# A fused attention and SoLU feed-forward kernel: one load of k moved ahead of two loads of v and a store, one transposing transfer moved ahead of a store

## The chip, the cores and the metric

The kernel runs on one core of a Trainium2 chip. A core has a matrix engine (TensorE; PE in the profile, PEld for its weight loads), VectorE (DVE), ScalarE (ACT), GpSimd (POOL), and SyncE (SP), which in this kernel issues every DMA transfer, in one queue and in program order. The metric is the device time of one launch in microseconds (us), lower is better.

## The reference

For 8 batches of 8 heads (576 rows, head size 64) the reference computes a linear attention, and on its output a feed-forward layer with the SoLU activation and a layer norm:

```
q_s = softmax of q over the head dimension; k_s = softmax of k over the rows
kv  = einsum('bhsd,bhse->bhde', k_s, v)
x   = einsum('bhsd,bhde->bhse', q_s, kv), as 4608 x 512
h   = x @ w_in                       (512 -> 1024)
s   = h * softmax(h)
ln  = (s - mean) / sqrt(var + 1e-6) * g_ln
out = ln @ w_out                     (1024 -> 512)
```

All inputs and the output are float32.

## The kernel before

Work is cut into pieces, and each piece is a Python generator: at each `yield` it stops, and the next call emits its next few instructions. The string `ORDER` names the generators one after another; `K4*3` means three steps of K4, and a suffix such as `.v` puts a step's movable instruction on VectorE. Since scheduling is manual, ORDER is the program order, so each engine's instructions run in the order in which the steps name them, and SP's transfers too. An instruction whose input isn't ready holds up all that stand behind it on its engine. Where instructions on different engines depend on each other, semaphores are put in automatically.

A number in a name below is a batch (0 to 7) for the first five kinds, and a row tile of 128 output rows for the others (36 tiles; four or five per batch).

- `LKb` (`load_keys`, L248): one transfer of 1152 KB that brings the batch's k into the tile `km`. There is one such tile, so the transfer waits until the kv products of batch b-1 have read the old one.
- `Vbi` (`load_v`, L228): a transfer of 288 KB for one of four parts of v into `vm`. There is one `vm` too, so each waits for the kv products of the batch before.
- `Kb` (`keys`): the softmax of k and the kv product, 26 steps. Steps 1 to 3 take the maximum over the rows on VectorE (`khalf`, L445 and L447, one step each; then `ktop`, L449 and L450); then come the transposes of the maximum, the subtraction (L456), the exponential (L458), the products into `kv` (L470), the normalization and a power of two as scale. The last six steps split the result into two float16 halves in `bd`: for each half of the partitions a scaled copy on ScalarE (L499), a copy on ScalarE (L501) and the remainder on VectorE (L503).
- `Qba`, `Qbc` (`queries`): the softmax of q for two row tiles, split into float16 halves in `qhl` (L547 computes the low half on GpSimd). The last step is only a transposing transfer, `qT<-qhl` (L574, on SP).
- `LQb` (`load_queries`): loads of q.
- `xt` (`attend`, L665): the attention product of two row tiles from `qT` and `bd`; then ScalarE and VectorE bring it out of PSUM.
- `Ht` (`hidden_twin`, L733): h = x @ w_in for two row tiles by seven block products. Its sums pass through the tile `vw`: ScalarE or VectorE copies a block out of PSUM into one half of `vw` (L171 or L173), VectorE adds it to another block and takes the maximum (L759, L769, L771), and a later copy overwrites the half. A product that adds onto a PSUM block can start only when the block has been copied.
- `ht` (`hidden`): softmax, product, mean and variance of a tile, ending in the transposing transfer `uT<-u` (L858).
- `ot` (`project`): 7 steps: a scale; four steps of products with w_out (L1117); the scaling out of PSUM into `os` (L1130 on ScalarE); the store to the output (L1133, on SP). Two `os` buffers are used in turn.

Around the first place of the change ORDER has, in order, V52, the last kv products of K4, V53, V50, the store of o7, LK5, the first two steps of K5, the last three steps of K4, the transposing transfer of Q4a and then a step of H15 whose first instruction is L759. Around the second place it has the store of o14 (the last of `o14*2`) and, eight steps on, the last step of Q5c.

Of the kernel before, what the change touches and what calls it, by code (L numbers as in the profile page):

```python
# [17 lines left out]
P = 128  # L18
# [27 lines left out]
}  # L46
ORDER = (
# [51 lines left out]
)  # L99


# [1153 lines left out]
```

## Time and profile before

| | us |
|---|---|
| median of 3 runs | 436.26 (436.16 to 440.52) |
| the profiled execution, device time | 436.4 |
| its span, first to last instruction | 434.6 |
| TensorE busy | 414.3 (95%) |
| VectorE busy | 379.2 (87%) |
| ScalarE busy | 333.5 (77%) |
| GpSimd busy | 315.1 (72%) |

The granted clock of TensorE is 1.0 of full speed in every slice of the span. The rows come from one profiled execution; start times are counted from the start of its span, which is 1.8 us shorter than its device time.

### The profile page before, as it was taken

The numbers are of one execution on the slowest core, as the hardware profiler recorded it, in microseconds if no ns is written. First come the engines' busy times: TensorE is split into PE (matmuls) and PEld (weight loads), VectorE is DVE, ScalarE is ACT, GpSimd is POOL, SyncE is SP. The second block draws the span as 40 slices with busy tenths as digits, with TensorE's granted clock in tenths as the row PEclk, the third lists the DMA queues.
The fourth block names the chain that finished last, engine by engine and source line by source line (L and its number), as shares of the span: only waits on it lengthen the run. The fifth ranks groups of instructions, "written<-read, shape, count | busy, mean of one in ns | idle before, by whom it ended". The sixth has DMA issues, their size and how long they took to land.

```text
span 434.6 us, 9274 instructions
## 1 busy us (share of the span) xinstructions
PE 414.3 (95%) x3473; PEld 221.0 (51%) x3473; DVE 379.2 (87%) x765; ACT 333.5 (77%) x566; POOL 315.1 (72%) x329
## 2 busy tenths in 40 slices
PE   2699999999999999989999999999999999999996
PEld 1444534454445444534544445445444558676885
DVE  5999999999889999976979968999999999896862
ACT  2789998786877889748865767898889878965830
POOL 4208765899899769848888799789998875687520
PEclk9999999999999999999999999999999999999999
DMA  8989895699897996687899686999424957769993
GB/s 275 409 308 330 180 200 137 123 220 226 180 203 146 238 206 136 157 159 160 184 201 205 92 205 117 278 228 120 110 50 97 142 104 137 151 136 183 167 229 113
DMA packets 185900, 78.72 MB, mean 181 GB/s; under 512 B 165240, under 2 KB 174720, under 8 KB 185856
## 3 DMA queue, kind: packets, MB, share of 16 engines
q1 hardware_dynamic: 185856, 78.14, 80.5%
q8 instruction: 27, 0.44, 0.4%
q14 instruction: 17, 0.14, 0.1%
HBM read 36.70 MB, written 9.44 MB: 106 GB/s over the span
## 4 chain that ended last, share of the span: by engine, by line
PE 73%; DVE 9%; DMA 8%; ACT 5%; issue 2%; SPq 2%; POOL 1%; DVEq 0%; ACTq 0%
PE o L1117 23%; PE h L733 19%; PE h L810 12%; PE kv L470 3%; DMA qm<-in_q_dram 3%; PE o_2y L1048 3%; PE x L665 2%; DMA km<-in_k_dram 2%; PE o_0y L1048 2%; PE o_2z L1048 2%; PE o_2x L1048 2%; DMA qT<-qhl 1%; PE o_0z L1048 1%; PE o_0x L1048 1%; DMA uT_2c<-u_2c 1%
## 5 line engine op out<-in xcount | busy, mean ns | idle before, releaser
L1117 PE MATMUL o<-wo,uT 128*128 128x512 f16 x576 | 130.8, 379 | 0.2 <-ACT os L1130 0.2
L1117 PEld LDWEIGHTS <-uT 128*128 128x128 f16 x576 | 55.1, 98 | 67.3 <-issue 2.9
L810 PE MATMUL h<-wi,xT 128*128 128x512 f16 x240 | 53.6, 379 | 0.0
L733 PE MATMUL h<-wt,split 128*128 128x512 f16 x198 | 46.1, 379 | 0.4 <-ACT vw L171 0.3
L547 POOL TENSOR_TENSOR qhl<-qm,qhl 128x512 f16<-128x512 f32 x28 | 34.5, 1250 | 15.5 <-ACT qhl L171 15.4
L733 PEld LDWEIGHTS <-split 128*128 128x128 f16 x264 | 25.5, 98 | 32.1 <-issue 2.8
L810 PEld LDWEIGHTS <-xT 128*128 128x128 f16 x240 | 23.3, 98 | 28.1 <-issue 0.7
L522 POOL TENSOR_TENSOR qm<-qm,qnmx 128x1024 f32<-128x1024 f32 (+1 forms) x15 | 28.6, 1915 | 6.2 <-DVE qnmx L520 5.9
L456 POOL TENSOR_TENSOR km<-km,kb 128x1152 f32<-128x1152 f32 x12 | 31.5, 2628 | 0.9 <-issue 0.6
L733 PE MATMUL h<-wi,xT 128*128 128x512 f16 x132 | 30.6, 379 | 0.0
L733 PEld LDWEIGHTS <-xT 128*128 128x128 f16 x198 | 19.2, 98 | 21.7 <-issue 0.4
L802 PE MATMUL h<-iw,xT 128*128 128x512 f32 x64 | 29.3, 599 | 0.9 <-ACT e L865 0.9
L540 POOL TENSOR_TENSOR qm<-qm,qrec 128x1024 f32<-128x1024 f32 x13 | 25.0, 1921 | 2.9 <-DVE den L477 1.0
L520 DVE TENSOR_REDUCE qnmx<-qm 128x16 f32<-128x1024 f32 (+1 forms) x17 | 19.2, 1144 | 3.9 <-DMA qm<-in_q_dram 3.9
L171 ACT COPY vw<-h 128x512 f32<-128x512 f32 x25 | 14.6, 584 | 9.9 <-DVE top L759 6.7
L824 ACT ACTIVATE e<-h,nm,hs 128x1024 f32<-128x1024 f32 x18 | 21.6, 1201 | 0.4
L524 ACT ACTIVATE qm<-qm 128x1024 f32<-128x1024 f32 (+1 forms) x17 | 17.0, 999 | 6.1 <-POOL qm L522 6.1
L470 PEld LDWEIGHTS kv<-vm,km 64*64 64x64 f32 x1152 | 18.0, 134 | 6.3 <-ACT km L458 3.1
L470 PE MATMUL kv<-vm,km 64*64 64x65 f32 x1152 | 19.5, 219 | 1.7 <-ACT km L458 1.6
L1130 ACT ACTIVATE os<-o,rr 128x512 f32<-128x512 f32 x22 | 15.1, 686 | 7.7 <-PE o L1117 7.2
L458 ACT ACTIVATE km<-km 128x1152 f32<-128x1152 f32 x16 | 18.2, 1161 | 2.9 <-POOL km L456 2.7
L865 ACT ACTIVATE e<-h,nmu 128x1024 f32<-128x1024 f32 x14 | 15.6, 1114 | 5.9 <-DVE u L855 5.7
(330 smaller groups left out, 1072.7 us busy)
## 6 DMA issues: line engine op xcount, KB each, us to landing
km<-in_k_dram SPq DMA_DIRECT2D x7, 1152.0 KB, 7.8
vm<-in_v_dram SPq DMA_DIRECT2D x28, 288.0 KB, 4.0
out_dram<-os SPq DMA_DIRECT2D x31, 256.0 KB, 3.0
qm<-in_q_dram SPq DMA_DIRECT2D x7, 1024.0 KB, 6.7
wo<-in_moe_w_in_dram SPq DMA_DIRECT2D x4, 512.0 KB, 8.5
w_in<-in_moe_w_in_dram SPq DMA_DIRECT2D x4, 512.0 KB, 9.2
wo<-in_moe_w_out_dram SPq DMA_DIRECT2D x4, 512.0 KB, 5.7
w_out<-in_moe_w_out_dram SPq DMA_DIRECT2D x4, 512.0 KB, 8.9
```

Source lines behind the costliest of these rows:

```text
L456: on(nc.gpsimd).tensor_tensor(km[:, ns], km[:, ns], wide, op=ALU.subtract)
L470: nc.tensor.matmul(o, km[half, n, c], vm[half, n, c], start=(m == 0 and c == 0), stop=(m == 1 and c == KC - 1))
L520: nc.vector.tensor_reduce(shaped(nmx), x, axis=AX.X, op=ALU.max, negate=True)
L522: on(nc.gpsimd).tensor_tensor(x, x, wide(nmx), op=ALU.add)
L540: on(nc.gpsimd).tensor_tensor(x, x, wide(rec), op=ALU.mult)
L547: on(nc.gpsimd).tensor_tensor(lo, y, hi, op=ALU.subtract)
L733: nc.tensor.matmul(out, lefts[left](s, i), right_block(right, r, i), start=(n == 0 and not onto), stop=(n + 1 == len(terms)), skip_group_c ...
L802: nc.tensor.matmul(h[:, ns], xT[:, kc], iw[kc][:, ns], start=(i == 0), stop=(i == NP - 1))
L810: nc.tensor.matmul(h[:, ns], xT[:, t, kc], wi[:, s, kc, ns], start=(i == 0), stop=(i == len(terms) - 1))
L824: nc.scalar.activation(e, h, AF.Exp, bias=nm, scale=hs, accum_out=z)
L1048: nc.tensor.matmul(accs[acc], t[:, j, first + f], out_block(right, s, f), start=(f == n == 0 and not onto), stop=(f + 1 == NF // 2 and n = ...
L1117: nc.tensor.matmul(o, uT[:, j, f], wo[:, s, f, cols], start=(f == 0 and j == 0 and s == 0), stop=(f == NF - 1 and j == 1))
```

## The change

Only the string ORDER is changed. LK5 moves from behind o7's store and K4's next-to-last group of steps to a place right behind the last kv products of K4, that is, in front of V53, V50 and the store of o7. The last three steps of K4, which stood behind the first two steps of K5, now stand in front of them. The store of o14 moves from in front of `h18.v` to behind the last step of Q5c, which is that batch's second transposing transfer of q. All other steps keep their order. Line breaks apart, the diff is:

```
-  x15 K4 V53 Q4c*2 x15 V50 Q4a*2 H13*3 Q4a K4*2 o11.v
+  x15 K4 LK5 V53 Q4c*2 x15 V50 Q4a*2 H13*3 Q4a K4*2 o11.v
...
-  x15 K4*5 H15*2 H15.v H15*2 K4 LK5 K5*2 K4*3 Q4c Q4a H15*3 K5
+  x15 K4*5 H15*2 H15.v H15*2 K4*4 K5*2 Q4c Q4a H15*3 K5
...
-  x22 o14*2 h18.v h18 K6.v H20 h19 o15 h18 x22 Q5c h19
+  x22 o14 h18.v h18 K6.v H20 h19 o15 h18 x22 Q5c o14 h19
```

## Rows read from the trace of the kernel before

**Rows 1.** The page, part 1: busy us, share of the span, instructions.
```profile
PE 414.3 (95%) x3473; PEld 221.0 (51%) x3473; DVE 379.2 (87%) x765; ACT 333.5 (77%) x566; POOL 315.1 (72%) x329
```
**Rows 2.** Waits of TensorE: waiting line, releaser, us in total, times, longest.
```profile
PE h L733 <- ACT vw L171: 2.1, 2, 1.8
...
PE x L665 <- DMA qT<-qhl: 0.5, 1, 0.5
```
**Rows 3.** Window: length, busy us PE, PEld, DVE, ACT, POOL, clock, DMA share, GB/s.
```profile
195.40:250.20 54.80, 54.80 (x421) 25.74 (x420) 47.32 (x109) 41.48 (x77) 45.25 (x50) 1.00 0.80 168
```
**Rows 4.** Chain that ended last, 172 to 206 us: start, us, what.
```profile
182.89 8.51 DMA km<-in_k_dram
...
194.76 0.59 ACT vw L171
```
**Rows 5.** Timeline of SP, 179 to 192 us: start, us, line, operation.
```profile
179.56 0.59 SPq L228 DMA_DIRECT2D vm<-in_v_dram  x1
...
180.20 1.71 SPq L228 DMA_DIRECT2D vm<-in_v_dram  x1
181.97 0.81 SPq L1133 DMA_DIRECT2D out_dram<-os  x1
...
183.39 7.90 SPq L574 DMA_TRANSPOSE qT<-qhl  x1
```
**Rows 6.** Timeline of VectorE, 188 to 195 us; in brackets idle before, and releaser.
```profile
188.53 1.00 DVE L503 SCALAR_TENSOR_TENSOR bd<-kvn,s_kv,bd 64x256 f16<-64x256 f32 x1 [0.30 <-ACT bd L499]
191.42 1.23 DVE L445 TENSOR_TENSOR khalf<-km 128x1024 f32<-128x1024 f32 x1 [1.90 <-DMA km<-in_k_dram]
192.68 0.69 DVE L447 TENSOR_TENSOR khalf<-khalf 128x512 f32<-128x512 f32 x1
193.41 0.48 DVE L503 SCALAR_TENSOR_TENSOR bd<-kvn,s_kv,bd 64x256 f16<-64x256 f32 x1
193.92 0.70 DVE L759 CUSTOM_DVE_ANT_0 h<-h,vw 128x512 f32<-128x512 f32 x1
```
**Rows 7.** Timeline of ScalarE near 189 us.
```profile
188.94 0.50 ACT L499 ACTIVATE bd<-kvn,s_kv 64x256 f16<-64x256 f32 x1
```
**Rows 8.** Timeline of TensorE, 192 to 198 us.
```profile
192.18 1.47 PE L733 MATMUL h<-wt,split 128*128 128x512 f16 x6
195.40 1.46 PE L733 MATMUL h<-wi,split 128*128 128x512 f16 x6 [1.75 <-ACT vw L171]
196.78 0.97 PE L665 MATMUL x<-qT,bd 128*64 128x256 f16 x16
```
**Rows 9.** Time to landing in three source views: L248 (k), L228 (v), L574 (qT).
```profile
DMA to landing us min/median/max: 5.3/7.4/8.5
...
DMA to landing us min/median/max: 3.2/4.0/9.4
...
DMA to landing us min/median/max: 4.3/4.7/9.9
```
**Rows 10.** Chain that ended last, 236 to 256 us.
```profile
243.83 0.69 ACT os L1130
...
245.01 5.73 DMA qT<-qhl
```
**Rows 11.** Timeline of GpSimd near 242 us.
```profile
241.71 2.28 POOL L547 TENSOR_TENSOR qhl<-qm,qhl 128x512 f16<-128x512 f32 x2
```
**Rows 12.** Timeline of TensorE, 248 to 252 us.
```profile
248.81 1.46 PE L733 MATMUL h<-wi,xT 128*128 128x512 f16 x6
250.78 0.97 PE L665 MATMUL x<-qT,bd 128*64 128x256 f16 x16 [0.51 <-DMA qT<-qhl]
```
**Rows 13.** Timeline of VectorE, 227 to 240 us.
```profile
227.28 1.48 DVE L445 TENSOR_TENSOR khalf<-km 128x1024 f32<-128x1024 f32 x1 [1.58 <-DMA km<-in_k_dram]
...
239.64 0.48 DVE L503 SCALAR_TENSOR_TENSOR bd<-kvn,s_kv,bd 64x256 f16<-64x256 f32 x1
```
**Rows 14.** Timeline of TensorE near 241 us.
```profile
241.42 0.97 PE L665 MATMUL x<-qT,bd 128*64 128x256 f16 x16
```

102 rows, old and new, of the table ORDER are left out of this document.

## The prediction

> **What bounds the kernel now.** I read the page first. TensorE is busy 414.3 of 434.6 us [rows 1], and the chain that ended last is TensorE's for most of its length: time can be won only where TensorE stands idle. So the next view is the list of what TensorE waited for. The longest are at the kernel's start, which the change doesn't touch; in its middle two waits are left [rows 2]: the product of `hidden_twin` (L733) for a ScalarE copy into `vw`, longest 1.8 us, and the attention product (L665) for the transfer of a `qT`, 0.5 us. A window from the end of the first to the start of the second says that nothing else is open between them: TensorE is busy for the whole 54.80 us [rows 3].
>
> The next views are the chain of waits at each place, and the engines' timelines around it. The first wait starts with the load of the sixth batch's k (`km`): it is issued at 182.89 and lands 8.51 us later, at 191.40 [rows 4]. SP could have issued it sooner. Its condition, the last kv product of batch 4, is met when V53 goes out at 179.56; then V50 (1.71 us) and a store (0.81) stand in front [rows 5]. On VectorE `khalf` (L445) sits idle 1.90 us for `km`, and behind it in program order come L447, a `bd` split (L503) and at 193.92 the maximum L759 [rows 6]. ScalarE may overwrite `vw` only then (194.76 [rows 4]), and TensorE, idle 1.75 us, goes on at 195.40 [rows 8].
>
> The second wait is SP's alone. The store of o14 waits for `os`, which ScalarE starts at 243.83, and only behind it Q5c's transposing transfer goes out at 245.01, to land 5.73 us later [rows 10]. GpSimd had its source `qhl` ready at 241.71 + 2.28 = 243.99 [rows 11]. TensorE idles 0.51 us [rows 12].
>
> **Part 1: LK5 in front of V53, V50 and o7's store; the last three steps of K4 in front of the first two of K5.** Nothing is added or removed; two queues see another order, SP's and VectorE's (ScalarE's share of K4 keeps its place among ScalarE's work).
>
> SP: `km` goes out at about 179.6 instead of 182.9. The nine loads of k take 5.3 to 8.5 us to land (median 7.4) [rows 9]; so this one lands between 184.9 and 188.1. V53, V50 and the store go out behind it, each later by its issue of about half a microsecond or by as long as the queue holds them back. V53 and V50 are read by the kv products of batch 5, which need that batch's whole chain of key steps first, and that chain begins with the very `khalf` of [rows 6]; this hides the delay.
>
> VectorE: the second L503 moves ahead of `khalf`. The first one ends at 188.53 + 1.00 = 189.53 [rows 6]; the second needs the L499 that ran on ScalarE from 188.94 for 0.50 [rows 7], so it can run at about 189.56, and with 0.48 it ends at 190.04. The new order is then 190.07 `khalf` (1.23), 191.33 L447 (0.69), 192.05 L759. That is 1.87 earlier than 193.92. Even the latest landing, 188.1, is 1.9 us ahead of `khalf`: k is off the path, and VectorE's own queue is what remains.
>
> ScalarE copies `vw` 0.84 us behind the start of L759 (193.92 to 194.76), TensorE follows 0.64 us later: 192.05 + 1.48 = 193.53. Without any wait TensorE would be there at 192.18 + 1.38 = 193.56, where 1.38 is the step from one group of six products to the next work, 195.40 to 196.78 [rows 8]. So the wait ends at the same time as the work before it: the gain is 195.40 - 193.56 = 1.84 us. It is a near tie, so bounds: one VectorE operation may take half a microsecond more, as the first L503 did beside the second (1.00 against 0.48 [rows 6]), which leaves 1.3; the plain durations of these very instructions are the nearest rows, so I take 1.84. At worst the load still lands at 191.4 and only L503 is out of the way (0.5), or another transfer pays for it (below zero; rival D).
>
> Later work must come forward with it. ScalarE, GpSimd and VectorE near 195 to 200 all stand behind this copy or behind TensorE's product, so they move too.
>
> The one transfer that a quicker TensorE may overtake is Q4a's: issued at 183.39, its issue lasting 7.90 us [rows 5], and landed 9.9 us after (the maximum of its kind [rows 9]), at 193.3. Its reader, the L665 group now at 196.78, would start at 194.9. That is 1.6 us of cover. The trace shows that this transfer, put behind k, was held until k was nearly in. The Trainium skill ("DMA: Bandwidth & Descriptors", section "Queues, rings and completion order") says that each DMA engine takes its descriptors in ring order; by that rule two pieces of v and a store now stand between k and this transfer, which is where rival D has its place. The row agrees with the rule as far as k is concerned. Against it counts that the same bytes stand ahead of the transfer before and after; only their order changes.
>
> **Part 2: Q5c's transfer in front of o14's store.** The transfer goes out at 244.0, when `qhl` is ready, not at 245.01. With its own 5.73 us it lands at 249.7, with the median of 4.7 [rows 9] at 248.7. TensorE without a wait would want it at 248.81 + 1.38 = 250.19 instead of 250.78 [rows 12]: gain 0.59 us, bounds 0.51 (the idle time as the row counts it) and 0. The store goes out some microseconds later; its `os` buffer is one of two, and the next output tile to be scaled (o15) writes the other, so a whole tile's projection hides the delay and I cost it at nothing; without that cover it would be the delay itself, up to the 5.73 us that the transfer takes. Since both sides of this race come forward by the same 1.84 us, the gains add.
>
> **Sum.** 1.84 + 0.59 = 2.43 us off the profiled execution's 436.4 (span 434.6, 1.8 around it): 434.0. The median of the runs shown, 436.26, is 0.14 lower; I leave that inside the range. This is 0.5%, below the 1% that a measurement of this kernel can tell from no change.
>
> **The rivals.**
> A. The forecast: both waits go and all later work moves, 433.4 to 434.6.
> B. Part of the first gain is taken back later. The next place where VectorE, not TensorE, sets the pace begins with LK6: `khalf` at 227.28 had waited 1.58 us for it, and VectorE is full from there on [rows 13]. If that load doesn't come forward, the `bd` split of batch 5 still ends at 239.64 + 0.48 = 240.12 [rows 13], while its reader, the L665 at 241.42 [rows 14], wants to start at 239.58: 0.54 us lost. With the tie of part 1 lost as well (0.54) the time is 436.4 - 2.43 + 1.1 = 435.1. For it: the transfer engines are 80% busy in this stretch [rows 3]. Against it: it is issued behind work of GpSimd that itself moves forward.
> C. The change doesn't do what it says: k, put ahead, shares its way with the pieces of v and still lands at about 191.4. Then L759 gains only the 0.5 of the L503 that no longer stands between, and part 2 remains: 436.4 - 0.5 - 0.59 = 435.3. Against it: that would be 11.8 us, 3.3 over the longest of nine.
> D. Slower. Place: the L665 group at 194.9, which waits for Q4a's transfer. V50, now behind k and V53, is held back on SP for as long as that transfer was (7.90 us [rows 5]): it goes out at about 180.8 and frees SP at 188.7, the store takes 0.8, and Q4a's transfer starts only at 189.5 instead of 183.39. With the median landing (4.7) it is there at 194.2 and costs nothing; with the 9.9 that it needed before, at 199.4, and TensorE stands 4.5 us: 436.4 - 2.43 + 4.5 = 438.5. It costs from a landing at 194.9 on and ends on the slower side from 197.3. For it: V50 was already held for 1.71 us with only V53 ahead, which itself took 0.59 [rows 5]. Against it: those 9.9 us were spent behind k, and k would be in by then.
> E. More than forecast: a small idle time further on goes too, 433.0.
>
> **How the numbers follow.** A 0.64, B 0.18, C 0.06, D 0.07, E 0.05. The predicted time is A's, 434.0. The range runs from E's edge, 432.9, to 436.6, which takes in B and C and leaves the larger part of D and surprises out. Faster by over 1% would be below 431.9, which no case gives: 0.02. Slower by over 1% would be above 440.6; D would need another 2.1 us: 0.03. Within 1%: 0.95.
>
> **What would show it.** Right: `km` of batch 5 issued near 179.6 and landed before 189; no idle time for DMA ahead of that `khalf`; the two rows of TensorE's waits [rows 2] gone or below 0.2 us; the transfer of Q5c issued within 0.1 us of `qhl`'s end; the end of the span 2.2 to 2.6 us earlier. Wrong: a wait of L665 for `qT` near 195 (D), a `khalf` that still waits for k (C), or TensorE idle between 230 and 290 (B).

## The result and the profile after

The changed kernel takes 433.86 us (median of 11 runs, 433.66 to 434.79); the kernel before, measured beside it, 437.89 (11 runs, 435.66 to 440.52). The ratio is 0.991, 95% interval 0.989 to 0.994. The profiled execution takes 433.8 us against 436.4, its span 432.0 against 434.6. The forecast was 434.0, that is a ratio of 0.994 to the profiled 436.4, just outside this interval: the measured gain is the larger one.

So the two profiled executions differ by 2.6 us, as forecast (2.43), but the two medians by 4.0. In 19 of 86 runs of the kernel before, taken over the three later measurements, the mean granted clock of TensorE was 0.996 or lower, and these are 19 of its 25 times above 437.3; for the 11 runs here, six of them above 437.3, the clock isn't on record.

In the changed kernel's own lines, numbers are two higher (L733 is L735, and so on). The waits of TensorE from 70 us to the end, which answer to [rows 2] (waiting line, releaser, us in total, times, longest):

```profile
PE h L735 <- ACT vw L173: 0.3, 1, 0.3
```

Both waits that the forecast was about are gone; the 0.3 us that is left lies near 349 us and was there before, as the shorter of the two waits in the first row of [rows 2]. The timeline of SP, which answers to [rows 5], and in the second fence k's landing from the DMA view (KB each, us from issue to landing):

```profile
175.67 0.60 SPq L230 DMA_DIRECT2D vm<-in_v_dram  x1
179.63 0.40 SPq L250 DMA_DIRECT2D km<-in_k_dram  x1
180.08 2.97 SPq L230 DMA_DIRECT2D vm<-in_v_dram  x2
183.09 3.57 SPq L1135 DMA_DIRECT2D out_dram<-os  x1
186.76 2.64 SPq L576 DMA_TRANSPOSE qT<-qhl  x1
```

```profile
km<-in_k_dram SPq DMA_DIRECT2D x1, 1152.0 KB, 7.0
```

k goes out at 179.63 and lands at 186.6. Behind it SP is held up: the two pieces of v take 2.97 us to issue, the store 3.57. VectorE's timeline (against [rows 6]) and, in the second fence, TensorE's (against [rows 8]):

```profile
188.54 1.53 DVE L505 SCALAR_TENSOR_TENSOR bd<-kvn,s_kv,bd 64x256 f16<-64x256 f32 x2 [0.29 <-ACT bd L501]
190.10 1.23 DVE L447 TENSOR_TENSOR khalf<-km 128x1024 f32<-128x1024 f32 x1
191.36 0.69 DVE L449 TENSOR_TENSOR khalf<-khalf 128x512 f32<-128x512 f32 x1
191.97 0.69 DVE L761 CUSTOM_DVE_ANT_0 h<-h,vw 128x512 f32<-128x512 f32 x1
```

```profile
192.19 1.47 PE L735 MATMUL h<-wt,split 128*128 128x512 f16 x6
193.50 1.46 PE L735 MATMUL h<-wi,split 128*128 128x512 f16 x6
194.89 0.97 PE L667 MATMUL x<-qT,bd 128*64 128x256 f16 x16
```

No bracket stands behind `khalf` any more: VectorE finds k there, 3.5 us after it landed, and what it waits for is its own queue. TensorE's group that started at 195.40 starts at 193.50, with its predecessor at the same time as before (192.18, now 192.19): 1.90 us gained.

The second place: the timelines of SP, of GpSimd (the low half of `qhl`) and of TensorE, a fence each, against [rows 10], [rows 11] and [rows 12]:

```profile
242.01 1.66 SPq L576 DMA_TRANSPOSE qT<-qhl  x1
243.76 1.20 SPq L1135 DMA_DIRECT2D out_dram<-os  x1
```

```profile
239.71 2.28 POOL L549 TENSOR_TENSOR qhl<-qm,qhl 128x512 f16<-128x512 f32 x2
```

```profile
246.91 1.46 PE L735 MATMUL h<-wi,xT 128*128 128x512 f16 x6
248.30 0.97 PE L667 MATMUL x<-qT,bd 128*64 128x256 f16 x16
```

The transfer goes out 0.02 us after its source is ready (239.71 + 2.28 = 241.99). The attention product starts at 248.30 instead of 250.78: 2.48 us, of which 1.90 came from the first place and 0.58 are new. That carries to the end, where the span is 2.6 us shorter.

### The profile page after: what moved, and what is told of

Same layout as the page of the kernel before. It is cut to its first block, busy times and chain, and to the rows that moved or that the text cites. A ratio compares the mean times of both kernels' runs of the same rounds, so it can differ in the third digit from the quotient of the medians.

```text
span 432.0 us, 9275 instructions
## 1 busy us (share of the span) xinstructions
PE 414.5 (96%) x3473; PEld 221.6 (51%) x3473; DVE 378.8 (88%) x765; ACT 333.6 (77%) x566; POOL 316.1 (73%) x329
## 4 chain that ended last, share of the span: by engine, by line
PE 82%; DVE 8%; DMA 3%; ACT 2%; issue 2%; POOL 1%; SPq 0%; DVEq 0%; ACTq 0%; POOLq 0%
PE o L1119 26%; PE h L735 21%; PE h L812 12%; PE kv L472 4%; PE x L667 3%; PE o_2y L1050 3%; PE o_2z L1050 2%; PE o_0y L1050 2%; PE o_2x L1050 2%; PE h L804 2%; PE o_0z L1050 1%; PE o_0x L1050 1%; DMA uT_2c<-u_2c 1%; DVE qnmx L522 1%; DMA qm<-in_q_dram 1%
## 5 line engine op out<-in xcount | busy, mean ns | idle before, releaser
L735 PE MATMUL h<-wt,split 128*128 128x512 f16 x198 | 46.1, 379 | 0.5 <-ACT vw L173 0.3
L735 PEld LDWEIGHTS <-split 128*128 128x128 f16 x264 | 25.5, 98 | 30.2 <-issue 0.8
L735 PE MATMUL h<-wi,xT 128*128 128x512 f16 x132 | 30.6, 379 | 0.0
L735 PEld LDWEIGHTS <-xT 128*128 128x128 f16 x198 | 19.2, 98 | 21.7 <-issue 0.4
```

What stands on the lines that cost most here:

```text
L735: nc.tensor.matmul(out, lefts[left](s, i), right_block(right, r, i), start=(n == 0 and not onto), stop=(n + 1 == len(terms)), skip_group_c ...
```

## The experiments

All kernels but the last group are the kernel before with another ORDER. "At full clock" are the runs with a mean granted clock of 0.998 or more.

| kernel | median (range), us | ratio to before [95%] | runs, of these below full clock | median at full clock |
|---|---|---|---|---|
| before, three measurements together | | | 86, 19 | 436.34 |
| both parts | 434.18 (433.73 to 435.02) | 0.994 [0.992, 0.996] | 9, 1 | 434.03 |
| part 1 | 434.58 (433.90 to 435.75) | 0.995 [0.993, 0.997] | 12, 0 | 434.58 |
| part 2 | 436.68 (435.06 to 439.30) | 1.001 [0.998, 1.003] | 12, 5 | 436.01 |
| load moved, no swap | 434.19 (433.63 to 434.29) | 0.993 [0.991, 0.996] | 7, 0 | 434.19 |
| swap, load not moved | 436.07 (435.06 to 438.53) | 0.997 [0.995, 0.999] | 12, 2 | 435.70 |
| V51 too in front of k | 438.63 (436.44 to 441.66) | 1.004 [1.001, 1.006] | 12, 8 | 436.80 |
| the same again | 436.70 (435.46 to 440.85) | 1.002 [0.999, 1.005] | 12, 4 | 436.26 |
| k behind V53 and V50 | 434.49 (433.90 to 437.44) | 0.995 [0.992, 0.997] | 12, 1 | 434.38 |
| V51 in front of Q4a's transfer | 434.11 (433.59 to 435.01) | 0.993 [0.991, 0.996] | 7, 1 | 434.07 |
| before, wait filled | 436.43 (435.84 to 437.85) | 1.000 [0.998, 1.002] | 12, 1 | 436.32 |
| V51 in front of k, wait filled | 436.77 (436.26 to 438.81) | 1.001 [0.999, 1.003] | 12, 0 | 436.77 |

**Both parts together**, measured beside the parts.

> Both parts of the change. Theory (two exposed waits removed): 433.9 us, profile as the changed kernel's: k of batch 5 lands near 186.6, no wait of TensorE between 70 and 290 us. Theory on spread: runs of the kernel before scatter over 435.7 to 440.5 because TensorE waits there for transfers whose landing varies; with both waits gone all runs lie within 1.2 us. Rival on spread: the scatter has another source, so it shows here too.

434.18 us with a scatter of 1.3 us (1.2 expected), beside a kernel before at 435.33 to 439.66. The difference of the full-clock medians is 436.34 - 434.03 = 2.31 us; that of all runs of this measurement is 436.42 - 434.18 = 2.24, so the 4.0 us of the first measurement did not come again. k landed at 180.80 + 5.7 = 186.5, the expected number, but that is a coincidence: in this trace all of this stretch runs 1.2 us later than in the changed kernel's, and the load took 5.7 us instead of 7.0. TensorE has no wait of more than 0.3 us between 70 and 433 us in it.

**Part 1 alone.**

```diff
-  x15 K4 V53 Q4c*2
+  x15 K4 LK5 V53 Q4c*2
...
-  K4 LK5 K5*2 K4*3 Q4c
+  K4*4 K5*2 Q4c
```

> Part 1 alone (k in front of V53, V50 and o7's store, the last steps of K4 in front of K5's first). Theory: 1.84 to 1.9 us below the kernel before's profiled 436.4, so 434.5; the wait of L665 for qT near 249 stays at 0.5 us. Rival (the store's place is what counts): 435.8 or more. Spread: small if k's landing is its source, as wide as before if the second wait is.

434.58. TensorE, timeline at the second place:

```profile
248.87 0.97 PE L665 MATMUL x<-qT,bd 128*64 128x256 f16 x16 [0.46 <-DMA qT<-qhl]
```

The wait for `qT` is still there, as expected (0.46 against 0.51 [rows 12]). The rival is out, since all 12 runs lie below its 435.8.

**Part 2 alone.**

```diff
-  x22 o14*2 h18.v h18
+  x22 o14 h18.v h18
...
-  x22 Q5c h19
+  x22 Q5c o14 h19
```

> Part 2 alone (Q5c's transfer in front of o14's store). Theory: 0.6 us below 436.4, so 435.8; k of batch 5 still lands near 191.4 and TensorE still waits 1.75 us near 195. Rival (the transfer would have been hidden once anything moves): no gain, 436.4. Spread: as wide as before if k's landing is its source.

In the trace it does what it should; TensorE's waits from 70 us on are one row:

```profile
PE h L733 <- ACT vw L171: 2.2, 2, 1.9
```

The wait for `qT` has gone, the one for `vw` stays. But the time, 436.68, can't be told from before (ratio 0.998 to 1.003): 0.6 us is lost in the scatter, and 5 of these 12 runs were below full clock. At full clock it is 436.01, 0.3 below the kernel before. The part's worth is read from the traces, 0.5 to 0.6 us (the wait that is gone, and the product that starts at 248.87 with part 1 alone and at 248.30 with both), not from these times. The five runs can't be the edit's doing if the clock falls near 197 us, as in the traces below, since the edit takes effect near 244; the kernel before beside it has 1 such run in 27. So the share of such runs seems to vary by itself.

**The load without the swap.**

```diff
-  x15 K4 V53 Q4c*2
+  x15 K4 LK5 V53 Q4c*2
...
-  K4 LK5 K5*2 K4*3 Q4c
+  K4 K5*2 K4*3 Q4c
```

> Only LK5 moved; K5's first two steps stay in front of K4's last three. Theory (the load is what was late, and VectorE's work ahead of L759 is the same in either order): khalf starts at 189.6, L759 near 192.0, the same 1.84 us as part 1 alone: 434.5. Rival (the swap of the steps carries the gain): L759 stays near 193.9, 436.4.

434.19, the whole gain. VectorE's timeline:

```profile
188.65 1.01 DVE L503 SCALAR_TENSOR_TENSOR bd<-kvn,s_kv,bd 64x256 f16<-64x256 f32 x1 [0.30 <-ACT bd L499]
189.59 1.21 DVE L445 TENSOR_TENSOR khalf<-km 128x1024 f32<-128x1024 f32 x1
190.83 0.69 DVE L447 TENSOR_TENSOR khalf<-khalf 128x512 f32<-128x512 f32 x1
191.55 0.48 DVE L503 SCALAR_TENSOR_TENSOR bd<-kvn,s_kv,bd 64x256 f16<-64x256 f32 x1
192.07 0.70 DVE L759 CUSTOM_DVE_ANT_0 h<-h,vw 128x512 f32<-128x512 f32 x1
```

With k there in time the order of the four operations hardly matters: L759 starts at 192.07 here and at 191.97 with the swap. The swap rival is out.

**The swap without the load.**

```diff
-  K4 LK5 K5*2 K4*3 Q4c
+  K4 LK5 K4*3 K5*2 Q4c
```

> Only the swap: the last three steps of K4 in front of K5's first two, LK5 where it was (behind o7's store). Theory: k still lands near 191.4 and khalf starts then, but the L503 of 0.48 us no longer stands between khalf and L759, so L759 starts at 193.4, TensorE waits 1.25 instead of 1.75 us: 435.9. Rival (the swap carries the gain): 434.5. Rival (nothing without the load): 436.4.

436.07, where 435.9 was expected; the interval (0.995 to 0.999) allows a gain of 0.3 to 2.1 us, and at full clock the medians differ by 0.6. Timelines of VectorE and of TensorE:

```profile
191.46 1.23 DVE L445 TENSOR_TENSOR khalf<-km 128x1024 f32<-128x1024 f32 x1 [1.37 <-DMA km<-in_k_dram]
```

```profile
194.75 1.46 PE L733 MATMUL h<-wi,split 128*128 128x512 f16 x6 [1.07 <-ACT vw L171]
```

`khalf` still waits for k; taking the 0.48 us of L503 out from behind it shortens TensorE's wait from 1.75 to 1.07 (1.25 expected). So the swap is worth something as long as k is late.

**The suspected cost doubled.**

```diff
-  K4 LK5 K5*2 K4*3 Q4c
+  K4 V51 LK5 K5*2 K4*3 Q4c
...
-  x18*2 V51 K5
+  x18*2 K5
```

> The suspected cost doubled: the kernel before with V51, another 288 KB, put in front of LK5. Theory: k goes out some 1.5 us later and lands near 193; TensorE's wait near 195 grows from 1.75 by as much, 3 to 3.5 us, and the time is 437.5 to 438.2. Rival (the load is hidden by something else): 436.4, no change.

The cost was not doubled: k went out at 183.26, 0.37 us later than in the kernel before and not 1.5, and landed near 192.5. The median, 438.63, is above what was expected all the same, and the trace shows why. TensorE's timeline in the kernel before and in this one, a fence each, and windows of this one (length, busy us of PE, PEld, DVE, ACT, POOL, granted clock, DMA share, GB/s):

```profile
197.69 2.76 PE L1117 MATMUL o<-wo,uT 128*128 128x512 f16 x12
200.29 1.46 PE L733 MATMUL h<-wt,xT 128*128 128x512 f16 x6
```

```profile
192.30 1.47 PE L733 MATMUL h<-wt,split 128*128 128x512 f16 x6
196.51 1.76 PE L733 MATMUL h<-wi,split 128*128 128x512 f16 x6 [2.75 <-ACT vw L171]
198.20 1.64 PE L665 MATMUL x<-qT,bd 128*64 128x256 f16 x16
199.77 3.33 PE L1117 MATMUL o<-wo,uT 128*128 128x512 f16 x12
202.93 1.46 PE L733 MATMUL h<-wt,xT 128*128 128x512 f16 x6
```

```profile
197.00:198.00 1.00, 1.00 (x5) 0.24 (x3) 0.87 (x3) 1.00 (x3) 0.53 (x1) 0.77 0.00 0
198.00:200.00 2.00, 2.00 (x18) 0.86 (x18) 1.57 (x5) 1.93 (x4) 2.00 (x3) 0.50 0.04 8
200.00:201.00 1.00, 1.00 (x4) 0.31 (x3) 0.00 (x0) 0.98 (x3) 0.82 (x3) 0.53 0.17 16
201.00:202.00 1.00, 1.00 (x6) 0.48 (x5) 0.94 (x1) 0.94 (x5) 0.92 (x3) 1.00 0.78 182
```

The wait grew by 1.0 us (1.75 to 2.75), in the theory's direction but short of its 3 to 3.5. Behind it the granted clock is 0.50, that is 1.2 instead of 2.4 GHz: the attention product takes 1.64 us where [rows 8] have 0.97, the next group 3.33 instead of the 2.76 that it takes in the kernel before. From 196.51 to the group that follows these, at 202.93, TensorE needs 6.42 us; in the kernel before it needs 4.89 (195.40 to 200.29). So 1.5 us are lost on top of the wait. That was expected by neither theory, and the 12 runs fall in two: four at full clock, 436.44 to 437.15, and eight below it, 438.56 to 441.66. The four are hardly slower than the full-clock runs of the kernel before beside them (median 436.80 against 436.57; in the repeat below eight runs, 436.26 against 436.12). So it isn't shown that these 288 KB cost their 1.0 us in every run: the theory of the wait is borne out by this trace, and by what moving k forward gave, not by the times of this kernel.

**k behind V53 and V50.**

```diff
-  x15 K4 LK5 V53 Q4c*2 x15 V50 Q4a*2
+  x15 K4 V53 Q4c*2 x15 V50 LK5 Q4a*2
```

(against the changed kernel)

> The changed kernel with LK5 behind V53 and V50, still in front of o7's store. Theory: k goes out near 182.0 and lands 7.0 to 8.5 us later, 189.0 to 190.5; VectorE is free for khalf only at 190.1, so the time is that of the whole change within 0.4 us: 433.9 to 434.3. Rival (k must stand ahead of the pieces of v): landing at 191.0 or later, 434.9 or more.

434.49, 0.3 above both parts together; timelines of SP and of VectorE:

```profile
181.91 0.94 SPq L248 DMA_DIRECT2D km<-in_k_dram  x1
```

```profile
190.28 1.23 DVE L445 TENSOR_TENSOR khalf<-km 128x1024 f32<-128x1024 f32 x1
```

k landed 8.3 us after its issue, at 190.2, and VectorE took it at 190.28, without a wait that the profile shows. So with the store alone gone from in front of it the load just makes it, and that with the help of the swap: without the swap VectorE would have been free for `khalf` at 189.59, as in the run of the load alone, and would have waited 0.6 us for k. It is on the edge: two of the 12 runs are at 436.69 and 437.44.

**More in front of Q4a's transfer (rival D).**

```diff
-  x15 V50 Q4a*2
+  x15 V50 V51 Q4a*2
...
-  x18*2 V51 K5
+  x18*2 K5
```

(against the changed kernel)

> Rival D of the prediction tried: the changed kernel with V51 put behind V50, so that 288 KB more stand in front of o7's store and Q4a's transposing transfer. In the changed kernel that transfer went out at 186.8 and landed at 191.3, 3.6 us ahead of its reader. Theory (queue order, a transfer waits for the bytes ahead of it and no longer): it lands 1.5 to 2.5 us later, 193 to 194, no wait, 433.9. Rival D: it lands after 194.9 and L665 near 195 waits for qT; each us of it is a us of time.

434.11, no wait. Timeline of SP:

```profile
180.36 5.20 SPq L228 DMA_DIRECT2D vm<-in_v_dram  x3
185.60 1.26 SPq L1133 DMA_DIRECT2D out_dram<-os  x1
186.96 3.12 SPq L574 DMA_TRANSPOSE qT<-qhl  x1
```

It landed 5.1 us after its issue, at 192.1, still 3 us ahead of its reader; that is 0.8 us later than in the changed kernel, less delay than the theory gave it. D is out at this size.

**Is it the clock?** Two kernels fill TensorE's wait with products whose result is overwritten, eight in the kernel before (below) and twelve in the one with V51 in front of k; the fill has to keep the engine busy without making anything earlier.

```diff
         product(t2[:, left], "s3", "t3", True)
         yield
+        for _ in range(8 if row_tiles[0] == tiles[15] else 0):
+            nc.tensor.matmul(t2[:, right], lefts["11"](0, 0), right_block("11", 0, 0), start=True, stop=True)
```

> The kernel before, with eight extra 128x512 products in the place where TensorE waits for vw near 194 (into a PSUM half that is overwritten afterwards; the output is unchanged), 1.7 us of work that only fills the wait. Theory (the runs of the kernel before above 437 are those in which TensorE's granted clock falls after this wait): no run has a mean clock of 0.996 or less for this reason, the fast end stays at 435.5 to 436.5, and the runs at 437.5 to 440 go, so the median is 436.0 to 436.5 with a scatter of 2 us or less. Rival (the scatter is the landing of k alone): the same scatter as the kernel before beside it.

> V51 in front of LK5, as in the run with the doubled cost, and twelve extra products (2.6 us) filling the longer wait. Theory (clock): all runs lie with that run's four at full clock, 436.4 to 437.3, the eight at 438.5 to 441.7 are gone. Rival (the price is the wait alone): median 438.6, scatter 5 us, as without the filling.

> The run with V51 in front of LK5 again, on the same chip as the two filled kernels: median 438.6, more than half of the runs at a mean clock of 0.996 or less and those 1.5 us or more above the others.

TensorE in the first of them, the kernel before with its wait filled (lines from L768 on are two higher):

```profile
193.46 1.89 PE L768 MATMUL h<-wi,xT 128*128 128x512 f16 x8
195.53 1.45 PE L733 MATMUL h<-wi,split 128*128 128x512 f16 x6 [0.18 <-ACT vw L171]
```

The group after the wait starts where it started before (195.53 against 195.40), so nothing is gained, and the median, 436.43, is that of the kernel before (436.41 beside it). But only one of 12 runs is below full clock, and with the longer wait filled none of 12. On the same chip 8 of 29 runs of the kernel before were, and 4 of 12 with V51 in front of k: 1 of 24 filled against 12 of 41 unfilled. That speaks for the clock, but it isn't proof: the kernel before taken alone has 1 of 12 against 8 of 29, and the runs of part 2 suggest that the share varies by itself.

The second filled kernel is no clean copy of the long wait either. VectorE and TensorE in its trace:

```profile
191.39 1.23 DVE L445 TENSOR_TENSOR khalf<-km 128x1024 f32<-128x1024 f32 x1 [1.87 <-DMA km<-in_k_dram]
```

```profile
196.08 1.46 PE L733 MATMUL h<-wi,split 128*128 128x512 f16 x6
```

k is there at 191.4 in spite of V51, as in the kernel before [rows 4], and it is the fill that holds TensorE until 196.08. The repeated kernel itself missed its expectation: its median is 436.70, not 438.6, because only a third of its runs lost the clock, not more than half; the four that did are at 438.26 to 440.85, the other eight at 435.46 to 437.05, so the split is the same and its share is not. Two runs of the filled V51 kernel lie at 438.42 and 438.81 at full clock: part of the scatter is something else, and was not followed up.

## Why the prediction was right

**Where the time was.** The reading of the two waits [rows 2] was right in place and size, and the window [rows 3] that showed nothing between them: in the trace after, TensorE is without a wait from 70 us to 349.

**Part 1.** The sum went step by step as it stood: k out at 179.63 (said 179.6), landed at 186.6 (184.9 to 188.1), `khalf` at 190.10 (190.07), L759 at 191.97 (192.05), the group behind the wait at 193.50 (193.56). Gain 1.90 us, said 1.84. The tie, VectorE's chain against TensorE's own queue, came out as a tie. The size that was off, by little, is TensorE's own step, 1.31 us (192.19 to 193.50) and not 1.38. One thing the prediction left open, which of its two edits does the work, the runs settle: the load alone brings all of it (434.19), the swap alone about 0.6 us at full clock.

**The cover of Q4a's transfer.** Rival D's first half came true in kind: SP was held behind k, so this transfer went out at 186.76, not at 183.39 (D had 189.5). Its second half didn't: the transfer landed 4.5 us after its issue, not 9.9, at 191.3, earlier than before. The DMA view of before and of after:

```profile
qT<-qhl SPq DMA_TRANSPOSE x1, 9.9
```

```profile
qT<-qhl SPq DMA_TRANSPOSE x1, 4.5
```

What the prediction held against D, that the 9.9 us were spent behind k, is what the traces show. In the eight in which this transfer went out with k still under way it landed 1.9 us after k (2.6 in the one with the store between them), 8.5 to 10.4 us after its own issue; in the five in which it went out only when k had landed, it took 4.5 to 5.3. The Trainium skill ("DMA: Bandwidth & Descriptors", "Queues, rings and completion order") has each engine take its descriptors in ring order; the traces agree as far as they show an order, since k lands ahead of this transfer in all thirteen.

**Part 2.** Transfer out at 242.01, 0.02 us behind its source; TensorE 0.58 us earlier than by part 1 alone (said 0.59). The store, now behind it, held TensorE up nowhere: there is no wait up to 349 us. This is shown by the traces; in the measured times part 2 alone can't be told from no change.

**The rivals.** B, a part lost in VectorE's full stretch, did not come: the next load of k moved with the rest. Timelines of VectorE at 225 and 238, against [rows 13], and of TensorE, against [rows 14]:

```profile
225.07 1.69 DVE L447 TENSOR_TENSOR khalf<-km 128x1024 f32<-128x1024 f32 x1 [1.38 <-DMA km<-in_k_dram]
...
237.64 0.49 DVE L505 SCALAR_TENSOR_TENSOR bd<-kvn,s_kv,bd 64x256 f16<-64x256 f32 x1
```

```profile
239.52 0.97 PE L667 MATMUL x<-qT,bd 128*64 128x256 f16 x16
```

All three are about 2 us earlier (2.21, 2.00 and 1.90). C fell with the landing at 186.6, D with the landing at 191.3 and the run with V51. E, a further idle time gone, did not come: the 0.3 us near 349 stayed.

**What the prediction lacked.** Its 434.0 is right, but the price of the wait was reckoned as its 1.75 us. In the profiled execution that is all; in about a fifth of the runs of the kernel before (1 of 27, 10 of 30 and 8 of 29 in the three measurements) the mean clock is lower too, and those cost 438.64 in the median against 436.34. The prediction set the scatter of the runs shown (436.16 to 440.52) aside. Removing the wait took most of it away: of the 46 runs of the five kernels with k ahead of v and the store, none is above 435.8. That the large scatter goes with the wait is shown; that it is the clock each time is not, since six of the 25 runs above 437.3 were at full clock. At full clock the change is worth 2.3 us, what was forecast; the 4.0 us of the first measurement fit a larger share of such runs in it, and with no clock on record for them that stays an inference.

## What to carry to other kernels

A load that waits only for a buffer belongs on its queue directly behind the event that frees the buffer; what stands in front of it on an in-order queue delays it, here by 3.3 us of issuing, and by a longer way to landing (5.5 to 7.0 us in the five traces with k in front of V53 and V50, 7.8 to 9.6 in the eight with k behind them). A transfer that nobody waits for should go behind. In a kernel bound by one engine, list that engine's waits and follow each back to an issue; two moved tokens in an order string were worth what the list said they were. A scatter of the runs is part of the profile too: the one profiled execution may show a wait at its mildest, and a wait of TensorE can cost more than its length in other runs, as in the trace with V51 in front of k.

## What the runs showed of the hardware that was not expected

TensorE's granted clock fell from 1.0 to 0.50 (2.4 to 1.2 GHz) behind a wait of 2.75 us in the trace with V51 in front of k, and behind one of 3.37 us when the same kernel was profiled again (0.50 from 197 to 200 there); behind 1.75 us in the profiled execution of the kernel before, and 1.90 in that of part 2, it stayed at 1.00. In the first of these traces it is back at 1.00 by 201. The Trainium skill ("TensorE: Matmul & The Clock Gate", "Part 1: The HAM clock gate") says that the gate passes half of the clock when TensorE has been idle; the two traces agree. That the runs of the kernel before with a mean clock near 0.995 lose theirs at the same place is inferred from the runs with the wait filled or removed, where such times become rare; none of them was profiled.

The three runs with k early that are below full clock are cheap, 435.02 us at most. One of them was profiled (both parts), and it lost the clock elsewhere (windows as above):

```profile
20.00:25.00 5.00, 3.87 (x95) 2.57 (x88) 4.70 (x12) 4.38 (x8) 1.57 (x1) 0.91 0.99 364
25.00:30.00 5.00, 5.00 (x13) 2.35 (x12) 5.00 (x6) 4.79 (x9) 0.00 (x0) 0.75 0.80 279
```

The clock falls there behind short waits of the start, the last three 0.69, 0.96 and 0.17 us long. In the changed kernel's trace the same waits are 0.49, 0.96 and 0.18, and the clock stays at 1.00; so these waits don't tell the two traces apart, and what made it fall here is open. The kernel takes 1 us more, not 2.3.

A second thing was SP: an issue isn't a fixed price. The same store took 0.81 us to issue in front of k [rows 5] and 3.57 behind it and two pieces of v; the transposing transfer took 7.90 and 2.64.
